# Opening of a kernel's last stage: first output weights decoded earlier, a freer chain to the first step, and that step in three passes

## Chip, cores and metric

The kernel runs on one core of one Trainium2 chip. The metric is the device time of one execution in microseconds (us), taken as the median of a few runs; less is better. One more execution was taken with the hardware profiler, and every row below comes from it.

## Reference

Three layers follow each other: causal attention, a soft mixture of experts, and a feed-forward layer with a cosine gate. The change touches only the seam between the second and the third.

```python
attn_out = _attn_ref(q, k, v)                 # 4 batches, 12 heads, 448 tokens, 64 wide
x = attn_out as (1792 tokens, 768)
# experts: 8 of them, 4 slots each, so 32 slots
logits = x @ phi
slot_input = softmax(logits over tokens).T @ x
for e in range(8):
    slot_out[e] = relu(slot_input[e] @ w1[e]) @ w2[e]
x = softmax(logits over slots) @ slot_out     # (1792, 768), rank 32
# last layer
h = x @ w_in                                  # (1792, 2048)
out = (h * cos(h)) @ w_out                    # (1792, 768)
```

The weights of the last layer, `w_in` and `w_out`, arrive as 64-bit floating-point numbers and are turned into 32-bit ones on the core.

## The kernel before

**Stages.** Attention fills the first 205 us, the experts go on to about 274 us, the last layer takes the rest. The experts read 48 weight pieces of 1 MB (`load_piece`, `next_piece`). The output of the last piece goes through ScalarE (`so`, line 773), two transposes on TensorE (778) and a VectorE copy (779) into `soT`, the slots' outputs. All of the last layer hangs on `soT`.

**The last layer.** Since x has rank 32, `x @ w_in` is computed as weights (32 slots by 2048) times slot probabilities (`CT`). The 2048 inner columns are 16 chunks of 128 (`fc`). Each chunk has an input item and an output item of weights of 768 KB; item numbers run in, out, in, out (item 0 is `w_in` of chunk 0, item 1 `w_out` of chunk 0). The 1792 tokens are blocks of 512, 512, 512 and 256. A step `s` is one chunk for one block, and there are 64 steps; `SEQ` lists them, so that few chunks are wanted early.

**Tasks, by letter.** For an item j: `ld` its load into one of four raw slots (line 677), `a` a scaling on ScalarE (684), `l`, `h`, `s` three VectorE passes over 768 words that put the 32-bit number together (687, 691, 695). The load of item j+4 waits for `s j`, since they share a slot. For an output item of chunk c: `u` (706, ScalarE) and `v` (719, GpSimd or VectorE) split the weights into a high and a low part. For a group q of one or two chunks: `wm` multiplies `soT` by the decoded input weights (794), `w4` copies it (802, ScalarE), `wr` repeats it over partitions (805, TensorE), `ws` and `wd` make its high and low parts (809 ScalarE, 813 VectorE). For a step: `H` (827) makes a block of h in bank 6 or 7, `Y`, `R`, `S`, `G` (831 ScalarE, 834 VectorE, 837 ScalarE, 840 VectorE) make h * cos(h), `K` (843, ScalarE) and `L` (846, GpSimd) its high and low parts. `B` is the step's output product: for each of six banks m three matmuls of 512 columns, high weight times high part (853), low weight times high part (854), high weight times low part (855). `F` empties a bank when a block's run of chunks ends (859 to 865).

**Order.** A list-scheduling planner inside the kernel gives each task a cost, a key and its predecessors, and walks through time; each engine's instructions are then recorded in the order in which the plan started them. Nothing else sorts them: each engine runs its own list in that order and waits where an operand isn't there. Item 0 is decoded while the experts still run (`decode(0)` at piece 44); items 1, 2 and 3 are decoded after `soT` in the plan. `keep_warm(n)` issues n products of the identity that nobody reads (459); they stand after the last piece (2), after `wm 0` (6), after `wr 0` (5) and after `H 0` (12), 25 in all.

## Time and profile before

| | us |
|---|---|
| median of 3 runs | 560.85 (558.65 to 562.61) |
| profiled execution | 561.64 |
| its span, first to last instruction | 559.9 |
| TensorE busy, 3794 matmuls | 516.5 |
| VectorE busy | 369.7 |
| ScalarE busy | 318.6 |
| GpSimd busy | 159.2 |

The span is the time from the first to the last instruction; 1.7 us of the profiled execution lie around it. Busy times of engines overlap. A busy TensorE isn't one at its peak, and the profile's page gives the clock that TensorE was granted in each stretch.

### The profile page before, as it was taken

The page shows a single profiled execution, that of the slowest core. Times are in us where ns is not written, and L with a number is a line of the kernel's source. Part 1 is how long each engine was busy: PE and PEld are TensorE (multiplying, and loading weights), DVE is VectorE, ACT ScalarE, POOL GpSimd, SP SyncE. Part 2 cuts the span into 40 slices and gives each one's busy share as a digit, 9 for nine tenths or more (in the row PEclk, how much of TensorE's full clock was granted, in tenths as well). Part 3 has the DMA queues.
Part 4 walks back from the last instruction along what each step waited for, and adds up shares of the span by engine and source line. Part 5 has one row for each costly group of instructions (what it writes and reads, how often), then busy time and mean ns, then how long its engine had stood idle before and what let it go on. Part 6 is the DMA issues. An engine that isn't in the chain of part 4 may idle for free.

```text
span 559.9 us, 10301 instructions
## 1 busy us (share of the span) xinstructions
PE 516.5 (92%) x3794; PEld 387.3 (69%) x3794; DVE 369.7 (66%) x918; ACT 318.6 (57%) x737; POOL 159.2 (28%) x195
## 2 busy tenths in 40 slices
PE   4999999989999998887779989999989999999997
...
GB/s 180 167 258 258 184 155 252 172 248 179 235 166 219 248 325 414 420 418 420 332 156 176 50 170 60 167 76 151 101 72 221 57 10 48 112 1 113 114 1 57
DMA packets 23954, 100.28 MB, mean 179 GB/s; under 512 B 2656, under 2 KB 6624, under 8 KB 17760
## 3 DMA queue, kind: packets, MB, share of 16 engines
...
## 4 chain that ended last, share of the span: by engine, by line
PE 51%; DMA 19%; DVE 13%; ACT 12%; issue 3%; SPq 0%; ACTq 0%; DVEq 0%
DMA w<-in_w_dram 10%; PE bank L853 8%; PE bank L854 8%; PE bank L855 8%; PE bank L295 7%; PE bank L328 5%; ACT p L308 5%; DMA zraw<-in_w_in_dram 5%; DMA zraw<-in_w_out_dram 4%; ACT pts L179 3%; DVE zscr L840 2%; PE bank L827 2%; PE bank L363 1%; DVE zfa L695 1%; PE bank L390 1%
## 5 line engine op out<-in xcount | busy, mean ns | idle before, releaser
L853 PE MATMUL bank<-zg,zhl 128*128 128x512 f32 (+1 forms) x384 | 142.4, 371 | 0.0
L855 PE MATMUL bank<-zg,zhl 128*128 128x512 f32 (+1 forms) x384 | 140.2, 365 | 0.4 <-POOL zg L846 0.4
L854 PE MATMUL bank<-zg,zhl 128*128 128x512 f32 (+1 forms) x384 | 140.3, 365 | 0.0
L846 POOL TENSOR_TENSOR zg<-zscr,zg 128x512 fp32r<-128x512 f32 (+1 forms) x64 | 81.6, 1278 | 155.4 <-ACT zg L843 124.3
L308 ACT ACTIVATE p<-p,pst 128x320 f32<-128x320 f32 (+3 forms) x168 | 87.6, 526 | 32.5 <-DVE pst L306 30.6
L325 POOL TENSOR_SCALAR p<-p,pst 128x320 f32<-128x320 f32 (+3 forms) x120 | 62.6, 539 | 131.2 <-ACT p L308 116.4
L853 PEld LDWEIGHTS bank<-zg,zhl 128*128 128x128 f32 x384 | 73.0, 190 | 12.7 <-issue 1.4
L855 PEld LDWEIGHTS bank<-zg,zhl 128*128 128x128 f32 x384 | 72.9, 190 | 12.7 <-POOL zg L846 0.9
L854 PEld LDWEIGHTS bank<-zg,zhl 128*128 128x128 f32 x384 | 73.0, 190 | 11.4
L306 DVE CUSTOM_DVE_ANT_0 p<-bank,cs 128x320 f32<-128x320 f32 (+3 forms) x168 | 66.9, 448 | 16.4 <-PE bank L295 12.6
L328 PE MATMUL bank<-cs,p 128*128 128x128 f32 (+1 forms) x456 | 59.8, 277 | 3.1 <-ACT pts L179 2.9
L834 DVE SCALAR_TENSOR_TENSOR zscr<-zscr,bank 128x512 f32<-128x512 int32 (+1 forms) x64 | 39.4, 618 | 34.1 <-ACT zscr L831 33.7
L837 ACT ACTIVATE zscr<-zscr,b_h 128x512 f32<-128x512 f32 (+1 forms) x64 | 42.6, 669 | 27.7 <-DVE zscr L834 27.5
L328 PEld LDWEIGHTS bank<-cs,p 128*128 128x128 f32 (+1 forms) x456 | 49.6, 134 | 11.3 <-issue 9.5
L840 DVE TENSOR_TENSOR zscr<-bank,zscr 128x512 f32<-128x512 f32 (+1 forms) x64 | 39.6, 621 | 22.0 <-ACT zscr L837 21.8
L295 PE MATMUL bank<-qk 64*128 64x192 f32 (+2 forms) x288 | 48.3, 471 | 5.4 <-DVE pst L306 5.4
L843 ACT ACTIVATE zg<-zscr 128x512 fp32r<-128x512 f32 (+1 forms) x64 | 36.8, 576 | 28.6 <-DVE zscr L840 28.3
L831 ACT ACTIVATE zscr<-bank,b_q 128x512 int32<-128x512 f32 (+1 forms) x64 | 40.2, 630 | 22.1 <-PE bank L827 21.9
L295 PEld LDWEIGHTS bank<-qk 64*128 64x128 f32 x288 | 27.2, 196 | 26.3 <-issue 10.3
L179 ACT ACTIVATE pts<-bank 128x512 f32<-128x512 f32 x71 | 40.5, 591 | 3.8 <-PE bank L328 2.3
L684 ACT ACTIVATE zraw<-zraw 128x768 f32<-128x768 f32 x32 | 28.9, 910 | 23.4 <-DMA zraw<-in_w_in_dram 15.6
L719 POOL TENSOR_TENSOR zhl<-uacc,zhl 128x768 fp32r<-128x768 f32 x4 | 8.8, 2204 | 98.6 <-ACT zhl L706 98.6
...
## 6 DMA issues: line engine op xcount, KB each, us to landing
...
```

The lines of the kernel that those rows point to most:

```text
L179: ACT.activation(o, i, AF.Copy)
L295: PE.matmul(sreg(j, c), lhsT=Q(p)[h, q0:q0 + 128], rhs=K(p)[h, 0:ln], start=True, stop=True)
L306: DVE.tensor_tensor_reduce(out=dst, in0=sb, in1=m, scale=-0.125, scalar=3.0e38, op0=ALU.add, op1=ALU.min, accum_out=st_[:, col:col + 1])
L308: return pr(f"exp{j}{c}")(lambda: ACT.activation(dst, dst, AF.Exp, bias=st_[:, col:col + 1], scale=-1.0, accum_out=st_[:, 8 + col:9 + col]))
L325: ENG[CFG["norm"][3 * j + c if c < 3 else 6]].tensor_scalar(dst, dst, st_[:, 24 + col:25 + col], 0.0, op0=ALU.mult, op1=ALU.add)
L328: PE.transpose(out, src, by)
L837: ACT.activation(y_(s), y_(s), AF.Sin, bias=b_h, scale=1.0)
L840: DVE.tensor_tensor(y_(s), hb[:, 0:n_(s)], y_(s), ALU.mult)
L846: eng.tensor_tensor(g_(s)[1], y_(s), g_(s)[0].bitcast(F32), ALU.subtract)
L853: PE.matmul(o, lhsT=wh, rhs=gh, start=first, stop=False)
L854: PE.matmul(o, lhsT=wl, rhs=gh, start=False, stop=False)
L855: PE.matmul(o, lhsT=wh, rhs=gl, start=False, stop=last)
```

## The change

It has five parts. `decode(1)`, the four instructions of item 1, is called in the last expert piece, ahead of the copy of `so`, so it stands ahead of that copy on ScalarE and ahead of the `soT` copy on VectorE. Of the `keep_warm` products after the last piece one is left, and the fixed ones behind `wm 0`, `wr 0` and `H 0` are gone. In their place the planner adds single ones (task `kw`) where TensorE would stand idle before the first output product. The planner gets a rule (`chain_next`): on TensorE, ScalarE and VectorE a task outside the chain from `wm 0` to the first output product isn't started if it would run into the chain's next task on that engine. Step 0's output product becomes three passes over the six banks (`back0`): high by high for all six, then low by high, then high by low. And the planner's numbers change: the start of the stage is set out by hand (`TIMED`, `free`), input items are due 0.7 steps later (their key is `need - 1.5` where it was `need - 2.2`), and a load costs 2.4 where it cost 1.87.

```diff
+                if npc[0] == 48:
+                    decode(1)
                 ACT.activation(so, sb[:, 0:256], AF.Copy)
                 tb = bank[6]
                 if npc[0] == 48:
-                    keep_warm(2)
+                    keep_warm(1)
...
+    def back0(s, m):
+
+        k_ = (0, 1, None, None, None, 2)[m]
+        gh, gl = g_(0)
+        for m in range(6):
+            fc = seq[0][1]
+            PE.matmul(bank[m][:, 0:n_(0)], lhsT=w_blk(fc, int(k_ == 1), m), rhs=gl if k_ == 2 else gh, start=k_ == 0,
+                      stop=k_ == 2 and seq[0][3])
...
-        key = need[GRP[qof[c]][0]] - 2.2 if k_ == "i" else need[c] - 0
-        if j >= 1:
+        key = need[GRP[qof[c]][0]] - 1.5 if k_ == "i" else need[c] - 0
+        if j == 1:
+            task(("s", 1), dict(DMA=5.05), [], -2)
+        if j >= 2:
             if j >= NRAW:
-                task(("ld", j), dict(DMA=1.87), [("s", j - NRAW) if j > NRAW else None], j)
+                task(("ld", j), dict(DMA=2.4), [("s", j - NRAW) if j > NRAW else None], j)
...
-    task(("so",), dict(DMA=3.0), [], -1)
+    task(("so",), dict(DMA=5.199999999999999), [], -1)
...
+        if s == 0:
+            task(("B", 0, 0), dict(T=1.4), [("K", 0), ("u", 0)], .0)
+            task(("B", 0, 1), dict(T=1.4), [("B", 0, 0), ("v", 0)], .1)
+            task(("B", 0, 5), dict(T=1.4), [("B", 0, 1), ("L", 0)], .2)
...
-    free = dict.fromkeys("TADP", 0.0)
+    free = dict(T=6.0, A=5.6, D=5.95, P=3.0)
+    TIMED = {("so",): 0, ("s", 1): 0, ("raw", 2): 0, ("raw", 3): 0}
...
+    CHN = [("wm", 0), ("w4", 0), ("wr", 0), ("ws", 0), ("wd", 0), ("H", 0), ("Y", 0), ("R", 0), ("S", 0), ("G", 0), ("K", 0), ("B", 0, 0)]
+    isch = set(CHN)
+
+    def chain_next(e, now):
+
+        w = None
+        for x in CHN:
+            if x in done:
+                continue
+            d = [y for y in T[x][1] if y not in done]
+            if not d:
+                r = tr_[x]
+            else:
+                r = max([tr_[x]] + [est_.get(y, now) for y in d])
+            (xe, dur), = [(k_, v_) for k_, v_ in T[x][0].items()][:1]
+            if xe == e:
+                return r
+            est_[x] = max(now, r, free[xe]) + dur + LAT[xe]
+        return 1e9
...
+                if e in "TAD" and t not in isch and chain_next(e, now) < now + eng[e] - 0.05:
+                    continue
...
+                if e == "T" and ("wm", 0) in done and ("B", 0, 0) not in done and chain_next("T", now) > now + .3 and \
+                        not any(w_ < now + .3 and "T" in T[x][0] for w_, x in soon):
+                    plan.append((now, len(plan), ("kw",), e))
+                    free["T"] = now + .23
+                    moved = True
...
-    warm = {("wm", 0): 6, ("wr", 0): 5, ("H", 0): 12}
...
-            keep_warm(warm.get(t, 0))
```

The plan of the whole stage comes out anew, so order moves up to step 38. Three places are shown. First, TensorE from the last expert matmul on, before (bank_67 marks a `keep_warm` product, which the trace records as two rows; bank_70 and bank_71 are banks 6 and 7; the first bank_70 row is the transposes behind `so`; 32x128 is `wm`, 96x128 `wr`, `CT` is `H`):

```order
L459 MATMUL bank_67<-cs 128x128 x2
L778 MATMUL bank_70<-cs 128x128 x2
L794 MATMUL bank_70<-zfa,dT 32x128 x6
L459 MATMUL bank_67<-cs 128x128 x6
L805 MATMUL bank_70<-cs 96x128
L459 MATMUL bank_67<-cs 128x128 x5
L794 MATMUL bank_71<-zfa,dT 32x128 x6
L827 MATMUL bank_70<-CT,zWS 128x512
L459 MATMUL bank_67<-cs 128x128 x12
L805 MATMUL bank_71<-cs 96x128
L827 MATMUL bank_71<-CT,zWS 128x512
L827 MATMUL bank_70<-CT,zWS 128x512
```

And now:

```order
L459 MATMUL bank_67<-cs 128x128
L780 MATMUL bank_70<-cs 128x128 x2
L796 MATMUL bank_70<-zfa,dT 32x128 x6
L459 MATMUL bank_67<-cs 128x128 x2
L807 MATMUL bank_70<-cs 96x128
L459 MATMUL bank_67<-cs 128x128 x3
L829 MATMUL bank_70<-CT,zWS 128x512
L796 MATMUL bank_71<-zfa,dT 32x128 x6
L459 MATMUL bank_67<-cs 128x128 x2
L807 MATMUL bank_71<-cs 96x128
L459 MATMUL bank_67<-cs 128x128 x6
L829 MATMUL bank_70<-CT,zWS 128x512
```

`H 0` stands ahead of `wm 1` now, and the products nobody reads are 14 instead of 25, spread in other portions; `H 1` and `H 2` come directly ahead of step 0's product, and `H 3`, which stood there too, comes behind it.

Second, VectorE from the end of item 0 on (`uacc` is item 1, `zfa` with zraw_2279 item 2, `lt` item 3, `zfb` items 4 and 6, `dT` is `soT`, `zWS` is `wd`, `zscr` are `R` and `G`), before:

```order
L695 SCALAR_TENSOR_TENSOR zfa<-zraw_2277,zfa 128x768
L779 COPY dT<-bank_70 128x2x16
L687 TENSOR_SCALAR uacc<-zraw_2278 128x768
L691 SCALAR_TENSOR_TENSOR uacc<-zraw_2278,uacc 128x768
L687 TENSOR_SCALAR zfa<-zraw_2279 128x768
L695 SCALAR_TENSOR_TENSOR uacc<-zraw_2278,uacc 128x768
L691 SCALAR_TENSOR_TENSOR zfa<-zraw_2279,zfa 128x768
L695 SCALAR_TENSOR_TENSOR zfa<-zraw_2279,zfa 128x768
L813 TENSOR_TENSOR zWS<-bank_70,zWS 32x128
L687 TENSOR_SCALAR lt<-zraw_2280 128x768
```

And now:

```order
L695 SCALAR_TENSOR_TENSOR zfa<-zraw_2277,zfa 128x768
L687 TENSOR_SCALAR uacc<-zraw_2278 128x768
L691 SCALAR_TENSOR_TENSOR uacc<-zraw_2278,uacc 128x768
L695 SCALAR_TENSOR_TENSOR uacc<-zraw_2278,uacc 128x768
L781 COPY dT<-bank_70 128x2x16
L687 TENSOR_SCALAR zfa<-zraw_2279 128x768
L691 SCALAR_TENSOR_TENSOR zfa<-zraw_2279,zfa 128x768
L695 SCALAR_TENSOR_TENSOR zfa<-zraw_2279,zfa 128x768
L815 TENSOR_TENSOR zWS<-bank_70,zWS 32x128
L687 TENSOR_SCALAR lt<-zraw_2280 128x768
L836 SCALAR_TENSOR_TENSOR zscr<-zscr,bank_70 128x512
L687 TENSOR_SCALAR zfb<-zraw_2277 128x768
```

Item 1's three passes moved ahead of the `soT` copy; item 2's three still stand between that copy and `wd 0`; behind `R 0` the first pass of item 4 (`zfb`) now precedes `G 0`.

On ScalarE the same stretch now reads as follows (zraw is `a`, with 2278 item 1, 2279 item 2, 2280 item 3; `cs` from bank_68 is `so`, from bank_70 and bank_71 `w4`; `zhl` is `u`; `b_q` is `Y`, `zscr` from `zscr` is `S`, `zg` is `K`):

```order
L684 ACTIVATE zraw_2278<-zraw_2278 128x768
L775 ACTIVATE cs<-bank_68 128x256
L684 ACTIVATE zraw_2279<-zraw_2279 128x768
L804 ACTIVATE cs<-bank_70 128x128
L684 ACTIVATE zraw_2280<-zraw_2280 128x768
L811 ACTIVATE zWS<-bank_70 96x128
L706 ACTIVATE zhl_2600<-uacc 128x768
L833 ACTIVATE zscr<-bank_70,b_q 128x512
L804 ACTIVATE cs<-bank_71 128x128
L839 ACTIVATE zscr<-zscr,b_h 128x512
L811 ACTIVATE zWS<-bank_71 96x128
L845 ACTIVATE zg_2597<-zscr 128x512
```

`a 1` moved ahead of `so`; `u 0` moved from ahead of `ws 0` to behind it; `S 0` stood behind `ws 1` and `a 5`, and now only `w4 1` stands between `Y 0` and `S 0`.

Third, TensorE at group 3 (chunks 4 and 5), which step 11 needs first. Before, from `wm 3` to `wr 3`:

```order
L794 MATMUL bank_70<-zfa,dT 32x128 x12
L853 MATMUL bank_65<-zg_2594,zhl_2600 128x512
L854 MATMUL bank_65<-zg_2594,zhl_2600 128x512
L855 MATMUL bank_65<-zg_2594,zhl_2600 128x512
L853 MATMUL bank_66<-zg_2594,zhl_2600 128x512
L854 MATMUL bank_66<-zg_2594,zhl_2600 128x512
L855 MATMUL bank_66<-zg_2594,zhl_2600 128x512
L805 MATMUL bank_70<-cs 96x256
```

And now:

```order
L796 MATMUL bank_70<-zfa,dT 32x128 x12
L855 MATMUL bank_64<-zg_2597,zhl_2602 128x512
L856 MATMUL bank_64<-zg_2597,zhl_2602 128x512
L857 MATMUL bank_64<-zg_2597,zhl_2602 128x512
L807 MATMUL bank_70<-cs 96x256
L855 MATMUL bank_65<-zg_2597,zhl_2602 128x512
L856 MATMUL bank_65<-zg_2597,zhl_2602 128x512
L857 MATMUL bank_65<-zg_2597,zhl_2602 128x512
L855 MATMUL bank_66<-zg_2597,zhl_2602 128x512
L856 MATMUL bank_66<-zg_2597,zhl_2602 128x512
L857 MATMUL bank_66<-zg_2597,zhl_2602 128x512
L829 MATMUL bank_70<-CT,zWS 128x512
```

`wm 3` stood behind the first bank of step 8 and now stands behind all of step 8; between `wm 3` and `wr 3` there is one bank of three matmuls instead of two, and `H 11` and `H 12` follow two banks after `wr 3` (before, `H 11` came at the end of step 8). The other two-chunk groups move likewise, by two to five banks.

## Rows read from the trace of the kernel before

**Rows 1.** Waits of TensorE from 288.5 us on: total us, times, longest.
```profile
PE bank L827 <- DVE zWS L813: 2.9, 2, 2.0
PE bank L827 <- DVE zscr L840: 2.7, 3, 1.6
PE bank L805 <- ACT cs L802: 2.1, 2, 1.4
PE bank L794 <- DVE zscr L840: 1.1, 1, 1.1
PE bank L855 <- POOL zg L846: 0.4, 1, 0.4
```

**Rows 2.** Timeline of the opening: start, us, engine, line, operation, [idle before].
```profile
273.27 0.38 ACT L773 ACTIVATE cs<-bank 128x256 f32<-128x256 f32 x1 [9.19 <-PE bank L771]
...
274.76 0.19 DVE L779 COPY dT<-bank 128x32 f32<-128x32 f32 x1 [7.85 <-PE bank L778]
...
275.65 1.60 PE L459 MATMUL bank<-cs 128*128 128x128 f32 x12
...
275.77 0.28 ACT L802 ACTIVATE cs<-bank 128x128 f32<-128x128 f32 x1
...
277.09 0.38 PE L805 MATMUL bank<-cs 128*96 128x128 f32 x2
...
278.61 0.26 ACT L809 ACTIVATE zWS<-bank 96x128 fp32r<-96x128 f32 x1
...
278.73 0.96 DVE L695 SCALAR_TENSOR_TENSOR zfa<-zraw,zfa 128x768 int32<-128x768 int32 x1
...
279.71 0.29 DVE L813 TENSOR_TENSOR zWS<-bank,zWS 32x128 fp32r<-32x128 f32 x1
...
280.30 0.50 PE L827 MATMUL bank<-CT,zWS 96*128 96x512 f32 x1
...
281.83 0.69 DVE L834 SCALAR_TENSOR_TENSOR zscr<-zscr,bank 128x512 f32<-128x512 int32 x1
...
284.68 0.71 ACT L837 ACTIVATE zscr<-zscr,b_h 128x512 f32<-128x512 f32 x1
...
286.15 0.63 ACT L843 ACTIVATE zg<-zscr 128x512 fp32r<-128x512 f32 x1 [0.18 <-DVE zscr L840]
...
288.59 0.40 PE L853 MATMUL bank<-zg,zhl 128*128 128x512 f32 x1
...
294.08 0.39 PE L855 MATMUL bank<-zg,zhl 128*128 128x512 f32 x1
...
294.31 0.39 PE L853 MATMUL bank<-zg,zhl 128*128 128x512 f32 x1
```

**Rows 3.** Line 677 (`ld`) between 253 and 256 us: the issue of item 1.
```profile
L677 SPq DMA_DIRECT2D zraw<-in_w_out_dram x1: 328/328/328, 253.8 to 253.8; - x1
...
DMA to landing us min/median/max: 19.2/19.2/19.2
```

**Rows 4.** Same timeline: GpSimd's `v 0` and VectorE's `l 3` beside it.
```profile
278.78 2.60 POOL L719 TENSOR_TENSOR zhl<-uacc,zhl 128x768 fp32r<-128x768 f32 x1 [84.51 <-ACT zhl L706]
...
280.04 1.76 DVE L687 TENSOR_SCALAR lt<-zraw 128x768 int32<-128x768 int32 x1
```

**Rows 5.** Stretches: length, busy PE, PEld, DVE, ACT, POOL, PEclk, DMA share, GB/s.
```profile
274.00:275.00 1.00, 0.73 (x4) 0.33 (x3) 0.24 (x2) 0.55 (x2) 0.00 (x0) 0.50 1.04 430
...
290.00:291.00 1.00, 1.00 (x4) 0.74 (x3) 1.00 (x3) 1.00 (x2) 0.41 (x1) 0.50 0.72 283
```

**Rows 6.** Timeline near 298 and 302 us: the issue of `ld 8` (x2: with `ld 10`), and `a 8`.
```profile
297.75 2.39 SPq L677 DMA_DIRECT2D zraw<-in_w_in_dram  x2
...
301.95 0.91 ACT L684 ACTIVATE zraw<-zraw 128x768 f32<-128x768 f32 x1 [2.76 <-DMA zraw<-in_w_in_dram]
```

**Rows 7.** Timeline near 419 and 425 us: `H 28` and `L 28`.
```profile
419.01 0.50 PE L827 MATMUL bank<-CT,zWS 96*128 96x512 f32 x1 [1.97 <-DVE zWS L813]
...
425.17 1.29 POOL L846 TENSOR_TENSOR zg<-zscr,zg 128x512 fp32r<-128x512 f32 x1
```

More of the change, by code (lines that the diff above doesn't have):

```diff
@@ L895, in moe_stack_kernel @@
             task(("v", c), dict(P=1.9, D=.9), [("u", c)], key - .6, True)
-    task(("so",), dict(DMA=3.0), [], -1)
+    task(("so",), dict(DMA=5.199999999999999), [], -1)
     for q, grp in enumerate(GRP):
-        key = need[grp[0]] - 2.2
+        key = need[grp[0]] - 1.5
         n = len(grp)
@@ L914, in moe_stack_kernel @@
         task(("L", s), dict(P=.07 + 1.2 * w, D=.07 + .55 * w) if LD else dict(P=.07 + 1.2 * w), [("K", s)], s - 1.5, True)
+        if s == 0:
+            task(("B", 0, 0), dict(T=1.4), [("K", 0), ("u", 0)], .0)
+            task(("B", 0, 1), dict(T=1.4), [("B", 0, 0), ("v", 0)], .1)
+            task(("B", 0, 5), dict(T=1.4), [("B", 0, 1), ("L", 0)], .2)
         for m in range(6):
+            if s == 0:
+                if last:
+                    task(("F", s, m), dict(D=.61) if m % 2 == 0 else dict(A=.5), [("B", 0, 5)], s + .2 + m / 10)
+                    pb[m] = ("F", s, m)
+                continue
             pv_ = ("B", s, m - 1) if m else (("B", s - 1, 5) if s else None)
@@ L927, in moe_stack_kernel @@
             succ.setdefault(x, []).append(t)
-    free = dict.fromkeys("TADP", 0.0)
+    free = dict(T=6.0, A=5.6, D=5.95, P=3.0)
+    TIMED = {("so",): 0, ("s", 1): 0, ("raw", 2): 0, ("raw", 3): 0}
+    for t, x in ((("raw", 2), 4.9), (("raw", 3), 6.8)):
+        T[t] = (dict(DMA=x - .9),) + T[t][1:]
+    CHN = [("wm", 0), ("w4", 0), ("wr", 0), ("ws", 0), ("wd", 0), ("H", 0), ("Y", 0), ("R", 0), ("S", 0), ("G", 0), ("K", 0), ("B", 0, 0)]
[15 more added lines that the diff above has]
+        return 1e9
+    done, est_ = set(), {}
     free["DMA"] = 0.0
@@ L932, in moe_stack_kernel @@
     pool, plan, hbf, hbo, now = [], [], [0.0, 0.0], {}, 0.0
-    while len(plan) < len(T):
+    while len(done) < len(T):
         pool += [t for w_, t in soon if w_ <= now + 1e-9]
@@ L948, in moe_stack_kernel @@
                     continue
+                if e in "TAD" and t not in isch and chain_next(e, now) < now + eng[e] - 0.05:
+                    continue
                 if e in "TAD" and any(w_ < now + LA * eng[e] and T[x][2] < key - KD and e in T[x][0] for w_, x in soon):
@@ L958, in moe_stack_kernel @@
             st_ = max(now, port["P" if e == "D" else "D"]) if pt and e in port else now
-            if t[0] == "so":
+            if t in TIMED:
                 fin = eng[e]
@@ L973, in moe_stack_kernel @@
             pool.remove(t)
+            done.add(t)
             plan.append((now if e != "DMA" else now, len(plan), t, e))
@@ L985, in moe_stack_kernel @@
     bk = lambda t: bank[6 + hbo[t]]
-    run = dict(ld=ld, a=dec_a, l=dec_l, h=dec_h, s=dec_s, u=up_part, S=t_s, K=t_k, B=back)
+    run = dict(ld=ld, a=dec_a, l=dec_l, h=dec_h, s=dec_s, u=up_part, S=t_s, K=t_k, B=lambda s, m: (back if s else back0)(s, m))
     run.update(H=lambda s: t_h(s, bk(("H", s))), Y=lambda s: t_y(s, bk(("H", s))), R=lambda s: t_r(s, bk(("H", s))),
@@ L990, in moe_stack_kernel @@
         run[nm] = lambda q, fn=fn: fn(q, bk(("wm", q)))
-    warm = {("wm", 0): 6, ("wr", 0): 5, ("H", 0): 12}
     with tc.manual_schedule():
         for _, _, t, e in plan:
-            if t[0] in ("so", "raw"):
+            if t in TIMED:
+                continue
+            if t[0] == "kw":
+                keep_warm(1)
                 continue
```

## Prediction

> **What bounds the kernel now.** The last stage is a row of output products on TensorE, so I read first where TensorE waits there. From 288.5 us to the end it waits at five kinds of place, 9.2 us in all [rows 1], and 1.6 of these stand ahead of the first product (the longest one for line 840, at `H 3`). So 7.6 us of waits lie behind the first product, in a stage of 270 us: whatever makes the products start earlier goes to the end of the kernel, unless new waits among the 7.6 take it back. All of these are waits for decoded input weights (`wd`, `w4`, the bank that `G` frees), never for more than 2.0 us at a time.
>
> Then I read the timeline of the opening in order [rows 2]. The reader is to follow one chain: `so`, the `soT` copy (ends 274.95), `w4 0`, `wr 0`, `ws 0`, `wd 0`, `H 0`, `R 0`, `S 0`, `K 0` (ends 286.78), and the first product at 288.59. From `soT` to the end of `K 0` it takes 11.8 us, and much of that isn't work. `w4 0` ends at 276.05, but six `keep_warm` products (275.65 to 277.25) hold `wr 0` until 277.09: 1.0. `wr 0` ends at 277.47, but ScalarE starts `ws 0` at 278.61, behind `u 0`: 1.1. `ws 0` ends at 278.87 and `wd 0` starts at 279.71, behind `s 2` on VectorE: 0.8. `R 0` ends at 282.52 and `S 0` starts at 284.68, since `ws 1` stands ahead of it on ScalarE and waits for `wr 1`, which stands behind twelve `keep_warm` products: 2.2. With 0.3 at `R 0`, behind a slow `l 3` [rows 4], and 0.3 at `H 0`, behind `wm 1`, that is 5.7 of the 11.8. The bare chain is 6.1.
>
> Behind the chain TensorE does `H 3` (freed late) and starts; its first product takes 5.72 us from 288.59 to 294.31 [rows 2], while 18 matmuls 0.23 apart, as the last two rows there are, would take 4.1. In this stretch the granted clock is 0.50, the lower level, 1.2 GHz [rows 5], behind the idle time that `R 0` to `K 0` left. So 1.6 us is lost to the clock.
>
> **The change, part by part.** *Item 1 ahead of `soT`.* Its load is issued at 253.8 and lands 19.2 later, at 273.0 [rows 3]. The last expert matmul ends near 273.2, for `so` starts at 273.27. `a 1` now stands ahead of `so` and runs 273.0 to 273.9 (0.91, as `a 8` [rows 6]), so `so` moves from 273.27 to 273.95: 0.7 later. VectorE needs `l 1` (about 0.5, for `l 3` ended 0.4 behind `v 0`, which held it [rows 4]), then `h 1` after `a 1`, 273.95 to 274.9, and `s 1` to 275.9 (0.96 each, as `s 2` [rows 2]); only then comes the `soT` copy, which ends at 276.15 instead of 274.95. This part costs the chain **1.2**. What it buys lies behind: item 1's passes no longer stand in the chain.
>
> *The chain kept free.* From 276.15 the bare chain of 6.1 gives 282.25 for the end of `K 0`. What still stands in it, by the new order: the three passes of item 2 between `soT` and `wd 0` (2.5 with gaps, so they end at 278.7 where `ws 0` would let `wd 0` start at 278.3): 0.4. `a 3` ahead of `ws 0` on ScalarE, 0.9 from the end of `w4 0` on, while `wr 0` takes 0.5 of it: 0.4, of which I count 0.1, since the wait for item 2 covers the rest. Two `keep_warm` products of 0.27 each (1.60 for six) beside `w4 0`: 0.1. `l 4` between `R 0` and `G 0`: this is a new place. `l 3` took 1.76 while `v 0` ran on GpSimd [rows 4], and it ended 0.4 after `v 0`; `u 0` would now end near 279.3, so `v 0` runs from 279.4 to 282.0 and `l 4`, ready to start at 280.9, is held as `l 3` was. Bounds 0 (where `S 0` covers it) and 0.9; I take 0.6. Together 1.2, so `K 0` ends at 283.5 and, with `H 1` and `H 2` ahead of it, the first pass starts at about **283.6** instead of 288.59.
>
> That holds with TensorE at the upper level. Before, it is granted 0.50 around `so`, at 274 to 275 [rows 5], and `keep_warm` kept TensorE busy between the last matmul and there. Now one product is left there, and TensorE idles from about 275.1 to 276.2. If the lower level lasts through `wr 0` and the first products nobody reads, these double: 0.5 for `wr 0`, up to 1.0 by `H 0`. I take the middle, 0.5: **284.1**.
>
> *Three passes.* The first needs only `K 0` and `u 0`, the second `v 0` (282.0), the third `L 0` (as `L 28`, 1.3 behind `K 0` [rows 7]). Two passes take 2.8, so the third isn't held, while before the third matmul needed `L 0`. Worth about 0.4 on its own, as the first product had to wait for `H 3` anyway; the product ends at 284.1 + 4.1 = 288.2.
>
> *Then comes step 1*, whose second matmul needs `v 1`, so this is the next wait. By VectorE's new order there stand behind `G 0` (ends 282.8 to 283.4): `wd 1`, `h 3`, `R 1`, `R 2`, `l 6`, `G 1`, `s 3`, which is 0.3 + 0.96 + 0.7 + 0.7 + 0.5 + 0.7 + 0.96 = 4.8, plus 0.3 where `R 1` waits for `Y 1`: `s 3` ends at 287.9 to 288.5. `u 1` on ScalarE takes 0.9, `v 1`, moved from GpSimd to VectorE, about 1.0 (nearest: a pass over 768 words, 0.96), and `L 1` on GpSimd may hold it by up to 0.5. So the second matmul of step 1 comes at 289.8 to 290.9, where in the old spacing it came at 294.31 + 0.23. TensorE idles some 2 us ahead of it. **The opening gains 3.6 to 4.7 by these; 3.7 is taken**, near the lower end, since each hop between engines that I left out adds to the chain. It is not the 4.5 of the first pass, and the clock's 1.6 is in it (the new product follows closely spaced work).
>
> *The rest of the stage.* Total work stays; 64 steps of 18 matmuls. What changes are the waits, 7.6 before. By the new order I find these. (a) `H 4` stands behind one bank of step 3, and its `wd 2` behind `ws 2`, which ScalarE has behind `a 8`. `s 4`, which frees that slot, would end near 296.3; the load took 4.2 from its issue before (297.75 to `a 8` at 301.95 [rows 6]), so `a 8` ends at 301.4, and `H 4` starts at 302.4 where TensorE is ready at 301.0: 1.4. Before, the same `a 8` stood ahead of `w4 2` and cost as much (the 1.4 of line 805 [rows 1]). (b) Step 4's third matmul waited 0.4 for `L 4`; the cover between `H 4` and it shrinks by one bank, 0.7: 1.1. (c) `w4 3` stands behind `a 13`, whose load waits for `s 9`: 1.5 at `wr 3`, by the same 4.2; before, 1.1 was lost at `wm 3`. (d) For groups 3 to 8 there are now 6.6 to 7.3 us of other work between `H` and the matmul that needs its `L`. In before the chain is 7.4 from `H 28` to the end of `L 28` [rows 7]; without the waits of the opening `H 0` to the end of `K 0` would be 6.5 less 2.5, and with an `L` of 1.3 and its start that is 5.5. At 5.5 nothing is lost, at 7.4 some 0.3 each for six groups, 1.6; nearer to the loaded one, I take 1.5. (e) `wm` and `wr` of groups 5 to 7 come 3 to 5 banks, 2 to 3.5 us, later, so the waits of 2.0 and less that stood there (`H 28`) should go: 0, bound 2.0 each. Sum 5.5 against 7.6: **2.1 gained**. Bounds: with 5.5 for every chain and no load late, 1.1 remains and 6.5 is gained; with (e) at its bound, 3.9 is lost.
>
> **Sum.** 3.7 + 2.1 = 5.8 us off. The profiled execution took 561.64, of which 559.9 is span and nothing outside it changes; that gives 555.8. It stands 0.8 above the median of the runs, 560.85, and from the median the same gain gives about **555.2**.
>
> **Rivals.**
>
> *Clock low through the first step.* For it: only one product holds TensorE busy before `soT`, and fourteen instead of twenty-five follow. Against it: from 276.2 the new order leaves TensorE hardly a gap. If the lower level held until the end of step 0's product, the 18 matmuls would be 0.43 apart, near what 5.72 for that product in part shows: start 284.6, end 292.3, later than `v 1`, so step 1 starts at 292.3 and the opening gains 2.0 instead of 3.7: 556.9. The Trainium skill, "TensorE: Matmul & The Clock Gate", Part 1, calls the lower rate the default which recent activity releases, and this speaks against taking `keep_warm` out; the trace agrees in that TensorE stood at the lower level after it had idled.
>
> *The gain is taken back in the loads.* All the waits of [rows 1] are for decoded weights, whose loads wait for a slot; and `s 3`, which frees the slot of item 7, stands behind `G 1` in the new order as the sum has it, at 287.9 to 288.5; the load behind it can't start sooner. If decoding sets the pace until group 7, TensorE starts early only to wait more, and the end moves by what the last of these waits allow, 0 to 1.5: about 560. Against it: items 4 and 6 finish earlier in the new order because `s 1` and `s 2` end 1 to 2 us earlier, and VectorE has gaps.
>
> *Later groups make it slower.* Input items are due 0.7 steps later, so `w4` and `wr` of groups 5, 6 and 7 each have a load's landing (`a 22`, `a 26`, `a 30`) right ahead of them on ScalarE. The rest of the stage turns the opening's 3.7 into a loss when these three wait over 1.9 each, about as long as the longest now, with (a) to (d) as above. At 2.5 each it is 5.5 + 7.5 = 13.0 against 7.6, 5.4 lost and 3.7 gained: 562.6.
>
> *It does more.* With no chain late and the opening at its best, 4.7 + 5: 551.
>
> **How the numbers follow.** Forecast as summed, 552 to 557.5: 0.60. Clock: 0.12. Loads: 0.13. Slower: 0.08. More: 0.07. A measurement of this kernel tells about 1%, 5.6 us, from no change. The forecast lies right at that bound: half of its chance and all of "more" are faster by over 1%, 0.40 with some of the clock case at most, and I put 0.43; slower by over 1% is only the far half of the slower case, 0.05; the rest, 0.52, is within. The range reaches from 551.5, short of "more", to 560.3, which takes in the loads.
>
> **What would show it.** In the new profile: `so` 0.7 later and the `soT` copy ending near 276.1; `K 0` near 283.5; the first pass near 284 at the upper level; a wait of about 2 us at step 1's second matmul, on VectorE's line of `v`; waits at `H 4` behind `a 8`, at step 4 for `L 4` and at `wr 3` behind `a 13`, each 1 to 1.5; no wait of 2 us at `H 28`. The prediction is wrong if `l 4` holds `G 0` by over 1 us, if the clock stays at 0.50 beyond 282, or if the waits behind the first product add to over 9.

## The result and the profile after

| | before | after |
|---|---|---|
| median, same chip | 561.16 us (6 runs) | 555.59 us (6 runs) |
| profiled execution | 561.64 | 556.55 |
| its span | 559.9 | 554.8 |
| TensorE busy, matmuls | 516.5, 3794 | 516.5, 3772 |

The ratio of after to before is 0.9907 with an interval of 0.9885 to 0.9929: 5.2 us of 560.85 are gone, by 4.0 to 6.4. The forecast was 5.8 us.

The end of the last expert matmul is the zero for comparing executions; I call it z. It lies at 273.15 in the trace of before and at 274.46 in that of after: the last weight pieces landed 1.3 us later in this execution (271.9 to 275.5 in the other traces below). From z to the end of the span before took 286.71 and after 280.31, 6.4 less in one execution each, at the upper end of what the medians allow.

The timeline of the opening after, with the columns of [rows 2]. From `so` on the tasks stand two lines further down than in the kernel before (`so` 775, `wm` 796, `w4` 804, `wr` 807, `H` 829, `B` 855 to 857); 865 is the three passes of step 0, 459 the products nobody reads:

```profile
275.25 0.38 ACT L775 ACTIVATE cs<-bank 128x256 f32<-128x256 f32 x1
...
277.26 0.18 DVE L781 COPY dT<-bank 128x32 f32<-128x32 f32 x1
...
277.50 1.07 PE L796 MATMUL bank<-zfa,dT 128*32 128x128 f32 x12 [1.13 <-DVE dT L781]
...
278.49 1.22 PE L459 MATMUL bank<-cs 128*128 128x128 f32 x4
278.61 0.28 ACT L804 ACTIVATE cs<-bank 128x128 f32<-128x128 f32 x1 [1.36 <-PE bank L796]
...
279.51 0.63 PE L807 MATMUL bank<-cs 128*96 128x128 f32 x2
...
280.49 0.29 DVE L815 TENSOR_TENSOR zWS<-bank,zWS 32x128 fp32r<-32x128 f32 x1 [0.52 <-ACT zWS L811]
280.81 0.56 DVE L687 TENSOR_SCALAR lt<-zraw 128x768 int32<-128x768 int32 x1
281.08 0.77 PE L829 MATMUL bank<-CT,zWS 96*128 96x512 f32 x1
281.27 1.81 POOL L719 TENSOR_TENSOR zhl<-uacc,zhl 128x768 fp32r<-128x768 f32 x1 [86.32 <-DMA zraw<-in_w_out_dram]
...
283.21 0.56 DVE L687 TENSOR_SCALAR zfb<-zraw 128x768 int32<-128x768 int32 x1
...
284.81 0.63 ACT L845 ACTIVATE zg<-zscr 128x512 fp32r<-128x512 f32 x1 [0.59 <-DVE zscr L842]
...
285.72 4.26 PE L865 MATMUL bank<-zg,zhl 128*128 128x512 f32 x18
...
288.68 0.95 DVE L695 SCALAR_TENSOR_TENSOR lt<-zraw,lt 128x768 int32<-128x768 int32 x1
...
289.70 0.83 ACT L706 ACTIVATE zhl<-lt 128x768 fp32r<-128x768 f32 x1
...
290.57 1.41 DVE L719 TENSOR_TENSOR zhl<-lt,zhl 128x768 fp32r<-128x768 f32 x1 [0.33 <-ACT zhl L706]
290.59 0.50 PE L855 MATMUL bank<-zg,zhl 128*128 128x512 f32 x1 [0.37 <-ACT zhl L706]
...
292.03 0.50 PE L856 MATMUL bank<-zg,zhl 128*128 128x512 f32 x1 [0.94 <-DVE zhl L719]
```

Read it as the chain of [rows 2]: `so` at z + 0.79 (before 0.13), the `soT` copy ends at z + 2.98 (1.81), `wd 0` starts at 6.03, `K 0` ends at 10.98 (13.64), the first pass starts at 11.26 (15.44), and the 18 matmuls take 4.26 to the end of the last one (5.88, counted likewise). Then `s 3`, `u 1` and `v 1` follow each other and TensorE waits for them: step 1's second matmul comes at z + 17.57, before at 21.39, so it is 3.82 earlier. Before, `v 1` was no bound; it ended at z + 20.26, while the first product was still running:

```profile
291.18 2.23 POOL L719 TENSOR_TENSOR zhl<-lt,zhl 128x768 fp32r<-128x768 f32 x1 [0.77 <-ACT zhl L706]
```

So the 3.82 took both, an earlier first product and an earlier `v 1`: with `v 1` where it was, at most some 1.1 could have come through (an estimate, 21.39 less 20.26).

The clock after, in the columns of [rows 5]:

```profile
274.00:275.00 1.00, 1.00 (x10) 0.50 (x2) 0.56 (x1) 0.56 (x1) 0.00 (x0) 0.50 1.03 424
282.00:283.00 1.00, 1.00 (x14) 0.59 (x7) 0.39 (x1) 0.62 (x2) 1.00 (x1) 0.62 0.97 399
290.00:291.00 1.00, 0.63 (x2) 0.19 (x1) 0.67 (x2) 1.00 (x3) 1.00 (x1) 1.00 0.33 92
```

The lower level, 0.50, lasts through `wm 0`, `wr 0` and `H 0`, to about 282.7, z + 8.3; before it ended at z + 2. In return it does not come back at the first products, where before stood at 0.50 at 290 [rows 5].

The waits of TensorE after, in the columns of [rows 1]:

```profile
PE bank L829 <- DVE zscr L842: 1.7, 3, 0.8
PE bank L829 <- DVE zWS L815: 1.3, 2, 0.9
PE bank L856 <- DVE zhl L719: 0.9, 1, 0.9
PE bank L857 <- POOL zg L848: 0.8, 1, 0.8
PE bank L855 <- ACT zhl L706: 0.4, 1, 0.4
```

The two for `zhl` are step 1's; the rest, 4.05 with two of 0.13 and 0.09 that the view leaves out, stand behind it and answer to 7.7 before. The 2.0 at `H 28` [rows 7] is gone, and so are the waits at `wr` and `wm` of over 1 us.

### The profile page after: what moved, and what is told of

Its sections match the earlier page's. It is cut to its first block, busy times and chain, and to the rows that moved or that the text cites. A ratio compares the mean times of both kernels' runs of the same rounds, so it can differ in the third digit from the quotient of the medians.

```text
span 554.8 us, 10257 instructions
## 1 busy us (share of the span) xinstructions
PE 516.5 (93%) x3772; PEld 384.5 (69%) x3772; DVE 366.0 (66%) x910; ACT 318.2 (57%) x737; POOL 165.3 (30%) x203
## 4 chain that ended last, share of the span: by engine, by line
PE 52%; DVE 18%; ACT 15%; DMA 11%; issue 3%; POOL 0%; SPq 0%; ACTq 0%; DVEq 0%
PE bank L855 8%; PE bank L857 8%; PE bank L856 8%; PE bank L295 7%; PE bank L328 5%; ACT p L308 5%; DMA zraw<-in_w_out_dram 4%; DMA w<-in_w_dram 3%; ACT pts L179 3%; DMA zraw<-in_w_in_dram 2%; DVE zscr L836 2%; PE bank L756 2%; DVE zscr L842 2%; ACT zscr L839 2%; PE bank L829 2%
## 5 line engine op out<-in xcount | busy, mean ns | idle before, releaser
L855 PE MATMUL bank<-zg,zhl 128*128 128x512 f32 (+1 forms) x378 | 139.8, 370 | 0.4 <-ACT zhl L706 0.4
L856 PE MATMUL bank<-zg,zhl 128*128 128x512 f32 (+1 forms) x378 | 137.5, 364 | 0.9 <-DVE zhl L719 0.9
L857 PE MATMUL bank<-zg,zhl 128*128 128x512 f32 (+1 forms) x378 | 137.3, 363 | 0.8 <-POOL zg L848 0.8
L848 POOL TENSOR_TENSOR zg<-zscr,zg 128x512 fp32r<-128x512 f32 (+1 forms) x64 | 82.8, 1299 | 139.2 <-ACT zg L845 119.0
L855 PEld LDWEIGHTS bank<-zg,zhl 128*128 128x128 f32 x378 | 71.4, 189 | 13.8 <-issue 1.2
L856 PEld LDWEIGHTS bank<-zg,zhl 128*128 128x128 f32 x378 | 71.5, 189 | 12.4 <-DVE zhl L719 1.6
L857 PEld LDWEIGHTS bank<-zg,zhl 128*128 128x128 f32 x378 | 71.4, 189 | 12.6 <-POOL zg L848 1.3
L684 ACT ACTIVATE zraw<-zraw 128x768 f32<-128x768 f32 x32 | 29.3, 916 | 23.9 <-DMA zraw<-in_w_in_dram 11.8
L719 POOL TENSOR_TENSOR zhl<-uacc,zhl 128x768 fp32r<-128x768 f32 (+1 forms) x7 | 10.6, 1529 | 101.8 <-DMA zraw<-in_w_out_dram 86.3
```

What stands on the lines that cost most here:

```text
L848: eng.tensor_tensor(g_(s)[1], y_(s), g_(s)[0].bitcast(F32), ALU.subtract)
L855: PE.matmul(o, lhsT=wh, rhs=gh, start=first, stop=False)
L856: PE.matmul(o, lhsT=wl, rhs=gh, start=False, stop=False)
L857: PE.matmul(o, lhsT=wh, rhs=gl, start=False, stop=last)
```

## The experiments

Each ran beside the kernel before on one chip, but not all on the same one (before took 560.17, 560.56 and 562.11 there), so kernels are compared by the ratio and not by the medians. The first table gives the times, the second what the traces show (one execution each): us from z, the waits of TensorE from step 1's third matmul on, and the time from the start of step 2 to the end.

| kernel | median, us (runs) | ratio to before | interval |
|---|---|---|---|
| after | 555.59 (6) | 0.9907 | 0.9885 to 0.9929 |
| x1 old numbers | 557.78 (12) | 0.9964 | 0.9944 to 0.9984 |
| x2 numbers alone | 557.10 (12) | 0.9944 | 0.9923 to 0.9965 |
| x3 no passes | 555.03 (6) | 0.9905 | 0.9887 to 0.9923 |
| x4 item 1 behind | 556.14 (6) | 0.9923 | 0.9902 to 0.9944 |
| x5 no guard | 556.32 (9) | 0.9931 | 0.9906 to 0.9955 |
| x6 more warm | 555.14 (6) | 0.9910 | 0.9882 to 0.9938 |
| x7 step 1 in passes | 554.94 (6) | 0.9902 | 0.9877 to 0.9926 |
| x8 x6 and x7 | 555.60 (6) | 0.9907 | 0.9886 to 0.9928 |
| x9 old due time | 561.39 (12) | 1.0012 | 0.9987 to 1.0036 |
| x10 old load cost | 564.65 (12) | 1.0061 | 1.0036 to 1.0086 |
| x11 first pass of step 1 | 554.58 (6) | 0.9879 | 0.9850 to 0.9908 |
| x12 x6 and x11 | 554.56 (6) | 0.9883 | 0.9853 to 0.9913 |

| kernel | `K 0` ends | step 1, 2nd matmul | step 2 | waits | step 2 to end |
|---|---|---|---|---|---|
| before | 13.64 | 21.39 | 25.24 | 7.7 | 261.5 |
| after | 10.98 | 17.57 | 21.70 | 4.1 | 258.6 |
| x1 | 10.64 | 18.89 | 24.48 | 4.0 | 258.9 |
| x2 | 13.64 | 21.37 | 25.22 | 5.1 | 259.0 |
| x3 | 11.72 | 18.31 | 22.44 | 4.3 | 258.5 |
| x4 | 9.48 | 17.48 | 21.67 | 4.9 | 259.1 |
| x5 | 11.81 | 18.61 | 23.45 | 4.1 | 257.6 |
| x6 | 10.74 | 17.32 | 21.45 | 4.2 | 258.6 |
| x7 | 10.93 | 16.40 | 22.11 | 5.2 | 257.8 |
| x8 | 10.85 | 16.32 | 22.03 | 4.8 | 257.0 |
| x9 | 11.38 | 19.75 | 25.33 | 5.5 | 261.5 |
| x10 | 11.81 | 18.38 | 22.51 | 11.1 | 267.8 |
| x11 | 10.72 | 16.19 | 21.43 | 5.4 | 258.6 |
| x12 | 11.70 | 17.16 | 22.39 | 5.5 | 258.4 |

In x3, x10 and x12 item 1 landed late, so `so` came at z + 1.5 to 1.6; they are to be read 0.7 to 0.8 earlier, and x9, where it came at 1.2, by 0.4.

**The numbers and the opening apart.** x1 is the changed kernel with the planner's two numbers put back, x2 the kernel before with the two new ones.

The edit of x1, in the kernel after:

```diff
-        key = need[GRP[qof[c]][0]] - 1.5 if k_ == "i" else need[c] - 0
+        key = need[GRP[qof[c]][0]] - 2.2 if k_ == "i" else need[c] - 0
...
-                task(("ld", j), dict(DMA=2.4), [("s", j - NRAW) if j > NRAW else None], j)
+                task(("ld", j), dict(DMA=1.87), [("s", j - NRAW) if j > NRAW else None], j)
...
-        key = need[grp[0]] - 1.5
+        key = need[grp[0]] - 2.2
```

> The changed kernel with the planner's old numbers (input items due 2.2 steps ahead, a load at 1.87); the whole new opening stays. Additive theory (opening about 3.8 us, the rest from fewer waits behind it): 557 to 558.5, and the waits of TensorE behind step 1 back near 7 us. Rival, the opening does it all and the waits shrink by themselves: 555.6 as the changed kernel. Rival, the numbers do it all: 561, as the kernel before.

> The kernel before with the planner's new numbers alone. Additive theory: 558 to 559.5, the waits behind step 1 near 4 to 5 us and the opening as before. Opening does it all: 561. Numbers do it all: 555.6.

x1 keeps 2.0 of the 5.2 us, x2 alone gives 3.1, so the times add up; the traces say that the parts don't, and the waits of x1, 4.0, are not back near 7. In x1 `K 0` ends as early as in after, but `a 6` stands ahead of `u 1` on ScalarE and `v 1` on GpSimd, where it takes 2.25:

```profile
289.19 2.25 POOL L719 TENSOR_TENSOR zhl<-lt,zhl 128x768 fp32r<-128x768 f32 x1 [0.24 <-ACT zhl L706]
...
291.49 0.50 PE L856 MATMUL bank<-zg,zhl 128*128 128x512 f32 x1 [1.83 <-POOL zhl L719]
```

TensorE waits 1.83 in one piece, the granted clock falls to 0.50 for some three us behind it, and at step 2 only 0.8 of the opening's 3.5 is left. In x2 the opening is as before. What lies behind step 2 shrinks by 2.6 in x1 and 2.5 in x2, and by no more, 2.9, in both together. So the new numbers do two things: with the old opening they shorten the rest, and with the new one, whose rest is nearly as short without them, they put `u 1` and `v 1` where that opening pays.

**One number at a time.** x9 puts only the due time back, x10 only the load's cost.

```diff
-                task(("ld", j), dict(DMA=2.4), [("s", j - NRAW) if j > NRAW else None], j)
+                task(("ld", j), dict(DMA=1.87), [("s", j - NRAW) if j > NRAW else None], j)
```

That is x10; x9 has the other two pairs of x1's lines.

> The changed kernel with one of its two numbers back: input items due at need - 2.2 again, the load still costing 2.4. The new numbers took 3.1 us alone, and undoing both took 2.0 from the change. The order that this plan gives puts a 6 ahead of u 1 on ScalarE and v 1 on GpSimd, as with both numbers old. Theory: the due time is the number that matters, by that order: step 1's second matmul near z + 18.9 (z: end of the last expert matmul), about 557.6 in all. Rival: the load's cost matters, since it sets where loads and a stand for the rest of the stage: then this is as the changed kernel, 555.6.

> The changed kernel with the other number back: a load costs 1.87 in the plan again, input items stay due at need - 1.5. Its order is the changed kernel's through the whole opening and differs from group 2 on. Theory (the due time matters): as the changed kernel, 555.6, second matmul of step 1 near z + 17.6, waits behind it some 4 us. Rival (the load's cost matters): about 557.6, with a above products that then wait for its load on ScalarE, and waits behind step 1 of 5 us and over.

Neither theory holds: x9 is as slow as before, x10 slower by 3.4 us. Each is worse than having both old. Step 1 in the timeline of x9, and its clock behind the two longest waits:

```profile
289.35 2.25 POOL L719 TENSOR_TENSOR zhl<-lt,zhl 128x768 fp32r<-128x768 f32 x1 [0.24 <-ACT zhl L706]
...
291.66 0.65 PE L856 MATMUL bank<-zg,zhl 128*128 128x512 f32 x1 [1.84 <-POOL zhl L719]
...
311.99 0.51 PE L857 MATMUL bank<-zg,zhl 128*128 128x512 f32 x1 [2.11 <-POOL zg L848]
```

```profile
292.00:293.00 1.00, 1.00 (x4) 0.71 (x4) 1.00 (x3) 0.85 (x1) 1.00 (x1) 0.50 0.00 0
313.00:314.00 1.00, 1.00 (x3) 0.72 (x3) 0.83 (x2) 0.36 (x2) 0.87 (x2) 0.50 0.00 0
```

The waits are for `v 1` and, at step 4, for an `L` on GpSimd that stood behind a `v` of 2.06. Behind each the matmuls follow 0.43 apart instead of 0.23. In x10 the opening is that of after; the loss lies behind it. Its waits at `wr`, and the rows ahead of the first of them:

```profile
PE bank L807 <- ACT cs L804: 4.8, 3, 1.9
```

```profile
333.31 0.91 ACT L684 ACTIVATE zraw<-zraw 128x768 f32<-128x768 f32 x1 [0.92 <-DMA zraw<-in_w_out_dram]
334.12 0.57 ACT L876 ACTIVATE zpx<-bank 128x512 f32<-128x512 f32 x1
334.59 0.37 ACT L804 ACTIVATE cs<-bank 128x256 f32<-128x256 f32 x1
...
335.01 0.67 PE L807 MATMUL bank<-cs 128*96 128x256 f32 x2 [1.83 <-ACT cs L804]
```

ScalarE stands idle for a load's landing with `a`, then empties a bank, and only then comes to `w4`, for which TensorE waits; at 390.96 and 421.50 it is an `a` with a landing and a `u` ahead of `w4`, 1.10 and 1.88. This is the mechanism of the rival "later groups make it slower", at groups 3, 5 and 6 where it named 5, 6 and 7, and at 1.1 to 1.9 a place where it asked for over 1.9. In after the waits at `wr` are 0.09 together, though the same `a` stands ahead of the same `w4` at the first place: its load was issued at z + 53.2 and had landed; in x10 it was issued at z + 56.1. What ScalarE waits for landings from step 1 on, in x10 and then in after:

```profile
ACT zraw L684 <- DMA zraw<-in_w_in_dram: 18.5, 12, 3.2
...
ACT zraw L684 <- DMA zraw<-in_w_out_dram: 5.0, 4, 1.9
```

```profile
ACT zraw L684 <- DMA zraw<-in_w_in_dram: 11.1, 7, 3.3
...
ACT zraw L684 <- DMA zraw<-in_w_out_dram: 1.9, 3, 0.7
```

23.5 stand against 13.0. This load takes some 4.2 from its issue (327.63 to the `a` at 331.86 in after at most, 329.16 to 333.31 in x10); the median of all these loads is 4.4 on the page of after. With 1.87 the plan takes it to be there sooner, sets `a` a few places earlier in ScalarE's row ahead of that group, and each wait there makes `s`, and with it the next load, later; this chain from one load to the next is argued from the later issue, 56.1 instead of 53.2, and was not followed through the stage. That the pair of numbers decides, and neither alone, is shown by the times. The 2.9 that x9 loses behind step 2 against after are its waits from there on, 5.5 instead of 4.1, and eight matmuls behind the wait of 2.11 that came 0.43 apart, which adds 1.4: together 2.8.

**The guard.** x5 takes the rule `chain_next` out of the planner.

```diff
-                if e in "TAD" and t not in isch and chain_next(e, now) < now + eng[e] - 0.05:
-                    continue
```

> The changed kernel without the rule that holds tasks back from the chain; everything else stays, the plan comes out anew. If the chain to the first pass sets when step 1 can go on: u 0, a 4 and a 5 stand in it again, the first pass comes 1 to 2 us later and the time is 556.5 to 557.5. Rival, the decoding up to v 1 sets it (s 3 and v 1 stand earlier on VectorE here): no later, 555 to 556.

It comes to 3.9 us gained against 5.2, between the two expectations, and the two intervals overlap widely. In the trace step 2 is 1.75 later: `u 0` stands ahead of `w4 0`, `H 0` starts 0.8 later, and `H 1` and `H 2` stand between the first pass and the other two, so that step 1's first matmul waits for `K 1`. Behind step 2 it is 1.0 better than after, which takes part of it back. The time alone doesn't show what the guard is worth.

**Item 1 behind `soT` again.** x4 takes `decode(1)` out of the last piece and gives its tasks to the planner, with the times set by hand moved along.

```diff
-                if npc[0] == 48:
-                    decode(1)
...
-    task(("so",), dict(DMA=5.199999999999999), [], -1)
+    task(("so",), dict(DMA=4.0), [], -1)
...
-    free = dict(T=6.0, A=5.6, D=5.95, P=3.0)
+    free = dict(T=4.8, A=3.4, D=4.75, P=3.0)
...
```

> The changed kernel with item 1 decoded behind soT again; guard, passes and numbers stay and the plan comes out anew (u 0 and v 0 late, v 0 on VectorE). Theory that decoding item 1 early pays: soT 1.2 us earlier, but l 1, h 1, s 1 and v 0 stand ahead of s 3 and v 1 on VectorE, so step 1's second matmul comes 1 to 2 us later and the time is 556.5 to 557.5. Rival, the 1.2 us that the early decoding costs the chain isn't earned back: 554.4.

In the trace `K 0` ends 1.5 earlier than in after, at z + 9.48, and step 1's second matmul comes at the same time, z + 17.48, for the same reason (854 is its line of that matmul):

```profile
288.54 0.84 ACT L706 ACTIVATE zhl<-lt 128x768 fp32r<-128x768 f32 x1
289.42 1.21 DVE L719 TENSOR_TENSOR zhl<-lt,zhl 128x768 fp32r<-128x768 f32 x1 [0.31 <-ACT zhl L706]
...
290.68 0.49 PE L854 MATMUL bank<-zg,zhl 128*128 128x512 f32 x1 [0.74 <-DVE zhl L719]
```

The same decoding passes are in the way, ahead of `soT` or behind it. The second matmul is not 1 to 2 us later, as the theory had it, and the time can't be told from that of after. In this trace the clock is at the upper level through the whole opening, so the 1.5 need not be the order's alone.

**Six more warming products.** x6 has three ahead of the last transposes and three behind them, where after has one.

```diff
-                    keep_warm(1)
+                    keep_warm(3)
                 for c in range(2):
                     PE.transpose(tb[:, 128 * c:128 * c + 128], so[:, 128 * c:128 * c + 128], ident)
+                if npc[0] == 48:
+                    keep_warm(3)
```

> The changed kernel with three products nobody reads ahead of the last two transposes and three behind them (one and none before), so that TensorE doesn't idle ahead of wm 0. If the clock matters: granted level 1.00 before 280 instead of 282.7, H 0 some 0.7 us earlier, and, since VectorE waited for ws 0 and for R 0, step 1 earlier by as much: 554.8 to 555.2. Rival, it stays at 0.50 or the chain isn't what step 1 waits for: 555.6.

The clock rises at z + 2.1 instead of 8.3 and `H 0` starts 0.87 earlier, but `K 0` ends only 0.24 earlier, step 1's second matmul 0.25, and the time can't be told from that of after. The rows between, of x6 (835 and 838 are its lines of `Y` and `R`):

```profile
280.05 1.82 POOL L719 TENSOR_TENSOR zhl<-uacc,zhl 128x768 fp32r<-128x768 f32 x1 [85.06 <-ACT zhl L706]
280.13 2.15 DVE L687 TENSOR_SCALAR lt<-zraw 128x768 int32<-128x768 int32 x1
...
280.69 0.69 ACT L835 ACTIVATE zscr<-bank,b_q 128x512 int32<-128x512 f32 x1 [0.72 <-PE bank L831]
...
282.31 0.69 DVE L838 SCALAR_TENSOR_TENSOR zscr<-zscr,bank 128x512 f32<-128x512 int32 x1
```

`v 0` now starts just ahead of `l 3`, which takes 2.15 instead of 0.56 and ends 0.4 behind it, as in [rows 4]; `R 0` waits for it, ready at 281.38 and started at 282.31. In after `wr 0` comes later, `wd 0` follows `ws 0` at once, and `l 3` (280.81) gets in ahead of `v 0` (281.27). The low clock's cost and this hold take each other's place. One execution is not enough to say what six products do to the clock, for the low stretch lies elsewhere in each: in x1 and x11, whose opening is that of after, it lasts from z + 3.3 to 6.7 and from 3.1 to 6.5. But all three traces with the six products (x6, x8, x12) are at the upper level from z + 2.1 to the first product, and all eight others with item 1 ahead of `so` are low at least from z + 3.3 to 6.5. And in all three `l 3` takes 2.13 to 2.15. Level or not, `K 0` ends between z + 10.5 and 11.0 in all eleven but x5, whose order is another (with the later `so` taken off).

**Step 0 bank by bank.** x3 takes the three tasks of step 0 out, so that it goes as every other step does.

```diff
-            task(("B", 0, 0), dict(T=1.4), [("K", 0), ("u", 0)], .0)
-            task(("B", 0, 1), dict(T=1.4), [("B", 0, 0), ("v", 0)], .1)
-            task(("B", 0, 5), dict(T=1.4), [("B", 0, 1), ("L", 0)], .2)
...
```

> The changed kernel with step 0's product bank by bank again, three matmuls each; the rest stays. Theory that step 1's wait for v 1 sets the pace: step 0 ends about 1.5 us later, since its third matmul waits for L 0, but step 1's second matmul comes no more than 0.3 later, and the time is 555.3 to 556. Rival, the passes bring what they let step 0 start earlier: 557.

It is as after, 0.9905, with step 2 at the same place once the 0.74 of the later `so` is taken off: the product ends later, but step 1 waits only 0.2 for `v 1` instead of 0.9.

**Without the wait at step 1.** x7 orders step 1 by passes of three banks (high by high, high weight by low part, low weight by high part), x8 adds the products of x6. x11 puts only the six high by high products first and then goes bank by bank, x12 adds the products of x6 to that.

The passes of x7 and those of x11 (the rest of either edit gives the planner the operands that each pass needs):

```diff
...
+        fc, k_ = seq[1][1], m // 2
+        for b in range(3 * (m % 2), 3 * (m % 2) + 3):
+            PE.matmul(bank[b][:, 0:n_(1)], lhsT=w_blk(fc, int(k_ == 2), b), rhs=gl if k_ == 1 else gh, start=False,
+                      stop=k_ == 2 and seq[1][3])
...
```

```diff
...
+        if m == 0:
+            for b in range(6):
+                PE.matmul(bank[b][:, 0:n_(1)], lhsT=w_blk(fc, 0, b), rhs=gh, start=False, stop=False)
+        for b in ((), (0, 1), (2,), (3,), (4,), (5,))[m]:
+            PE.matmul(bank[b][:, 0:n_(1)], lhsT=w_blk(fc, 0, b), rhs=gl, start=False, stop=False)
+            PE.matmul(bank[b][:, 0:n_(1)], lhsT=w_blk(fc, 1, b), rhs=gh, start=False, stop=seq[1][3])
...
```

> The changed kernel with step 1's product in passes as well: high by high, then high weight by low part, and the low weights (v 1) last; work is the same. Theory that step 1's wait for v 1 goes through to the end: TensorE goes on at u 1, the wait of 0.9 to 1.3 us is gone and the time is 554.3 to 554.8. Rival, it comes back behind (the banks that F must empty come free later, H 4 waits longer for its load): 555.6.

> The changed kernel with step 1 in passes and with the six products nobody reads around the last two transposes. If both count and add: 554 to 554.5. If only the passes count: as the run with them alone. If neither: 555.6.

> The changed kernel with step 1's high by high products of all six banks ahead of its other twelve, which then go bank by bank. With three passes by threes the wait for v 1 (0.94) went, but all banks ended late and step 2 waited 1.67 for the first of them to be emptied. Here v 1 has 1.4 us more, and bank 0 ends some 1.2 us later than in the changed kernel instead of 2.8 or more. Theory: the wait at v 1 goes and step 2 waits for nothing: step 2 begins near z + 20.8 instead of 21.7, and 554.7 in all, 0.9 less. Rival: the first bank's emptying stands late on VectorE anyway, or the waits behind take the gain back: step 2 again near z + 21.7, 555.6.

> The kernel of the run before with three products nobody reads ahead of the last two transposes and three behind them, as in the run that raised the clock 6 us earlier. Theory: the chain's part of the gain was hidden behind v 1 in that run (only 0.25 came through), so without that wait more of it does: step 2 near z + 20.3, 554.2 in all, 1.4 less than the changed kernel. Rival: u 1 on ScalarE, not v 1, sets step 1's start, and it does not move with the clock: as without the products, within 0.3.

In x7 the wait at `v 1` is gone and another stands behind step 1, since its banks all end late and step 2 needs the first emptied (line 881 is `F`):

```profile
291.53 4.37 PE L872 MATMUL bank<-zg,zhl 128*128 128x512 f32 x18 [0.34 <-ACT zhl L706]
...
297.57 0.47 PE L855 MATMUL bank<-zg,zhl 128*128 128x512 f32 x1 [1.67 <-DVE zraw L881]
```

In x11 the banks end earlier, but `F` of bank 0 stands behind a pass of item 4 or 6 on VectorE and starts at 293.26 (line 884):

```profile
292.40 0.94 DVE L691 SCALAR_TENSOR_TENSOR zfb<-zraw,zfb 128x768 int32<-128x768 int32 x1
293.26 1.28 DVE L884 COPY zraw<-bank 128x512 f32<-128x512 f32 x2
...
294.09 0.47 PE L855 MATMUL bank<-zg,zhl 128*128 128x512 f32 x1 [1.18 <-DVE zraw L884]
```

Of the 1.4 at step 1's second matmul 0.3 are left at step 2, and x12 waits for the same `F` as long, 1.18. x8 waits there 1.65, as x7 does, and has the ratio of after. By the traces the rivals in the expectations hold: the wait is moved. The times can't confirm that: x11 and x12 have the lowest ratios of all, but their intervals, which reach to 0.9908 and 0.9913, don't part them from after. All four beat the kernel before, none is shown to beat after.

**Not undone by itself.** No run puts the fixed products behind `wm 0`, `wr 0` and `H 0` back; what their going is worth is read off the traces, not tested.

## Why the prediction was right, point by point

*`decode(1)` ahead of `soT`: right in size.* 1.2 forecast for the copy's end, 1.17 measured; `so` 0.7 later, measured 0.66. x4 adds that it buys nothing measurable at step 1, and in four of the eleven traces with item 1 ahead (x3, x9, x10, x12) its landing cost 0.4 to 0.8 more.

*The chain: right in sum, by two terms that took each other's place.* From the copy's end to the end of `K 0` it took 8.00 (10.98 less 2.98). The forecast was 6.1 bare, 1.2 for what still stands in it and 0.5 for the clock, 7.8. The 0.6 for `l 4` did not come: it took 0.56 at 283.21, behind `v 0`, which ended at 283.08. Nor did the 0.4 for item 2: VectorE stood idle for 0.52 ahead of `wd 0`. The clock took more than 0.5: `wm 0` 1.07, `wr 0` 0.63, `H 0` 0.77 stand against 0.71, 0.38 and 0.50 before, 0.9 together; the products nobody reads ran slowly too and held `wr 0` by 0.6 (`w4 0` ended at 278.89) and `H 0` by 0.2, where 0.1 was forecast; and the clock stayed low to 282.7, which by z is 281.4 in the time of before, short of the 282 beyond which the prediction would be wrong. x6 showed why that did little harm: with the clock up, the hold that I had put at `l 4` comes at `l 3`, 0.9. That the sum came out within 0.2 is luck.

*Step 1's wait as the next bound: right, and the step that carried the forecast.* Second matmul 3.7 earlier forecast, 3.82 measured, by `s 3`, `u 1` and `v 1`. x3, x4 and x6 change the start of step 0 or its length and come out with step 1 at z + 17.3 to 17.6 (x3 with its later `so` taken off). That `v 1` follows this closely hangs on the planner's numbers, as x1 shows, and the prediction, which read it off the new order, gave the numbers no part in it. The wait itself was forecast near 2 and measured 0.37 and 0.94, as the first product ended 0.5 later than forecast and `H 3` and step 1's first matmul take up part of it.

*Three passes, 0.4: mis-sized.* x3 shows nothing. The passes only end the product earlier ahead of a wait.

*The rest, 2.1: right in sign, 2.9 measured* from step 2 to the end. The prediction read all waits of [rows 1] as waits for decoded weights; by the rows only the 2.9 and 2.1 are, the others are for the bank that `G` frees and, 0.4, for `L 4`. Of the terms in waits, 5.5 forecast and 4.05 measured: (a) `H 4` 1.4, measured 0.89. The rows are the following; `wd 2` behind `ws 2` behind `a 8` as forecast (the row names `l 7`, which ended just then, but the load of item 8, issued at 297.64, landed 4.3 later), and `H 4` comes at z + 29.3, as forecast (302.4 less 273.15), but TensorE gets there 0.5 later than I had it.

```profile
302.07 0.91 ACT L684 ACTIVATE zraw<-zraw 128x768 f32<-128x768 f32 x1 [1.48 <-DVE lt L687]
...
302.88 0.36 ACT L811 ACTIVATE zWS<-bank 96x256 fp32r<-96x256 f32 x1
...
303.28 0.42 DVE L815 TENSOR_TENSOR zWS<-bank,zWS 32x256 fp32r<-32x256 f32 x1 [1.25 <-ACT zWS L811]
...
303.75 0.73 PE L829 MATMUL bank<-CT,zWS 96*128 96x512 f32 x2 [0.89 <-DVE zWS L815]
...
310.08 0.50 PE L857 MATMUL bank<-zg,zhl 128*128 128x512 f32 x1 [0.84 <-POOL zg L848]
```

(b) `L 4` 1.1, measured 0.84. (c) `wr 3` 1.5, measured nothing: I had charged a landing to `a 13` and no wait is there. (d) six chains 1.5: wrong as a mechanism, for behind step 4 no matmul waits for an `L`; what stands there instead are 2.2 at five `H` (0.78, 0.39, 0.13, 0.59, 0.36), four of them for the bank that `G` frees. (e) 0, measured 0.09. So the sum of the waits came out near, by terms of which (c) and (d) were not there, which is luck again. Waits of 3.7 are gone by the view, and 2.7 of time from step 1's third matmul on; the rest are matmuls of 512 columns that followed later than 0.23 without a wait that the view counts, by 0.2 at most each, 6.0 together in after and 5.0 before. But (e) was right without a reason: I read the due time as what moves `wm` and `wr`, and gave the load's cost no part. x10 shows that with the due time alone these waits come, 4.8 at three places.

*The sum.* From the median, 560.85, the 5.8 give 555.05, not 555.2; the ratio makes it 555.6.

*The rivals.* The clock through step 0: no, the first pass is at the upper level. The gain taken back in the loads: no. Later groups: not in after, but real, as x10 shows. It does more: no.
